# An attention and two-layer kernel: the low part of x for the first eight units formed by TensorE and ScalarE, its loads and first products in another order

## The chip, the cores and the metric

The kernel runs on one core of a Trainium2 chip (trn2). The metric is device time in microseconds (us) of one execution; lower is better. Engines are named as the profile names them: PE (TensorE matmul), PEld (its weight loads), DVE (VectorE), ACT (ScalarE), POOL (GpSimd), SP (SyncE, which here only issues DMAs).

## What is computed

The reference, cut to what matters: a gated linear attention over four batches, eight heads, 768 positions and a head size of 48; its 3072 rows of 384 go through two feed-forward layers of width 2048.

```
state = alpha[:, :, t, :, None] * state + einsum('bhd,bhe->bhde', k[:, :, t], v[:, :, t])
y[:, :, t] = einsum('bhd,bhde->bhe', q[:, :, t], state)
...
x = y.transpose(0, 2, 1, 3).reshape(3072, 384)
h = x @ w_in;  g = maximum(0.01 * h, h);  x = g @ w_out            # layer 1
h = x @ w_in;  g = where(h > 0, h, exp(minimum(h, 0)) - 1);  out = g @ w_out   # layer 2
```

## The kernel before, in words

**Units and blocks.** The attention is cut into 24 units of 128 positions, six per batch; four units make a block of 512 rows of `x`, so layer 1 works on six blocks. A product in this kernel takes its operands as a high part (fp32r) and a low part (what is left): `hp` is summed over `wh*xh`, `wl*xh` and `wh*xl`, nine matmuls of 512 columns, and `y` in the same way, nine matmuls from `gh` and `gl`.

**A unit** `u` is computed in four pieces (function `quarter(u, i)`):
- piece 0: PE `pu(u)` (L231); DVE `prep_k(u+1)`: scan `E` (L127), `pe`, reciprocal, product into `pack` (L132); DVE `T(u)` (L187).
- piece 1: DVE mask `A(u)` (L180, two); PE transposes `pk(u+1)` (L166), ACT copy `kn(u+1)` (L173); PE `po(u)` from `A` (L212) and from `T` (L218).
- piece 2: DVE scan `F(u+1)` (L139), `S(u)` (L248), product (L144); PE scores `sc(u+1)` (L158); ACT `xh(u)`, the high part of x out of the PSUM tile `po` (L237); the loads of `pack` and `vt` of unit `u+3`, issued on ACT's queue (L111, L116).
- piece 3: DVE `xl(u) = po - xh` (L240); after a block's last unit also `gather`, six DMAs on SP's queue (L262) that move rows of `x` into place, without which that block's `hp` cannot start.

`sc`, `pk`, `pu` and `po` share three PSUM buffers in turn (pool `ps_a`), so `pu(u+1)` takes the buffer of `po(u)` and waits for the last reader of `po(u)`.

**Weights of layer 1** arrive as 64-bit words and are converted, 16 slices `m`. `stage1(m)` asks for the words of one slice with five DMAs on SP's queue (786 KB in all) into one of four buffers. Conversion of a slice is `p` (ACT, L270 and L271), `a` (DVE L275, L276, L278, then ACT L279, the high part) and `b` (DVE L282, the low part; then `stage1(m+4)`).

**Order.** Up to the end of the sixteen steps below, every engine runs in the order in which the code is written. First come units 0 to 3 with the conversion of slices 0 to 2 among them, then the start of unit 4 with the first two `hp` of block 0. Then sixteen steps `s`: PE `y` of slice `s`, PE `hp` of slice `s+2`, ACT `t` (L303), conversion `a` of slice `s+3`, pieces of units 4 to 7, DVE `max` (L308), ACT `gh` (L312), conversion `b`, DVE `gl` (L318), conversion `p` of the next slice. Of the thirteen pieces left, one is placed in each of the steps 1 to 13. After step 15 the rest (blocks 1 to 5 of layer 1 with units 8 to 23, then layer 2) is ordered by the framework's scheduler.

Of the kernel before, what the change touches and what calls it, by code (L numbers as in the profile page):

```python
# [19 lines left out]
def attention_two_layers_kernel(  # L20
# [40 lines left out]

    ident = const.tile([128, 128], F32, name="ident")
    causal = const.tile([128, C], F32, name="causal")
    d0 = const.tile([PR, EXT], F32, name="d0")
    d1 = const.tile([PR, EXT], F32, name="d1")
    bias = const.tile([PR, 2], F32, name="bias")
# [16 lines left out]

    def constants():
        make_identity(nc, ident)
        nc.gpsimd.memset(causal, 1.0)
        nc.gpsimd.affine_select(
            out=causal, in_=causal, compare_op=ALU.is_ge, fill=0.0,
            base=0, pattern=[[1, C]], channel_multiplier=-1,
        )  # L90
        nc.vector.memset(d0, 0.0)
        nc.vector.memset(d0[:, 0:EXT:C + 1], 1.0)
        nc.vector.memset(d1, 0.0)
        nc.vector.memset(bias[:, 0:1], -1.0)
        nc.vector.memset(bias[:, 1:2], -ALPHA_SPAN)
        nc.vector.memset(far_sum[:, 1:2], 1.0)
# [141 lines left out]

    def attn_xl(u, xh, xl, off):
        nc.vector.tensor_sub(xl[0:PR, :, off:off + C], st[u]["po"], xh[0:PR, :, off:off + C].bitcast(F32))  # L240

    def attn_state(u):
        c = u % NC
# [57 lines left out]
    def ffn1_t(j, m):  # L301
        t = g_p.tile([128, xt[j][2]], F32, tag="t", name="t")
        nc.scalar.activation(t, steps[1, j, m], ACTF.Copy, scale=0.01)  # L303
        steps[1, j, m] = t, steps[1, j, m]

    def ffn1_max(j, m):
        t, hp = steps[1, j, m]
        nc.vector.tensor_max(t, t, hp)  # L308
# [140 lines left out]
    def next_load(u):  # L449
        if u < NU:  # L450
            load_unit(u, eng=nc.scalar)
            load_v(u, eng=nc.scalar)
        else:
            t = pack_p.tile([128, 2 * 768], I32, tag="pack", name="stg")
            slots2.extend([(t[:, 0:768], 99), (t[:, 768:1536], 99)])
            fill2()
# [3 lines left out]
    def stage1(m, eng=None):  # L460
        t = x2t[m % 4].rearrange("p c f -> p (c f)").bitcast(I32)
        w = w_words[0][m]
        n = 2 * DM
        for j in range(2):
            nc.sync.dma_start(t[64 * j:64 * j + D, 0:n], w[D * j:D * j + D, 0:n])
            nc.sync.dma_start(t[64 * j + D:64 * j + 64, 0:n], w[PD + 16 * j:PD + 16 * j + 16, 0:n])
        nc.sync.dma_start(t[:, n:], w[:, n:])
        staged[1, m] = t
# [184 lines left out]
    with ExitStack():  # L653
# [5 lines left out]
        load_v(1)  # L659
        stage1(0)  # L660
        load_v(2)
        for m in range(1, 4):
            stage1(m)
        order1 = [("both", m) for m in range(KF)]
        conv1 = Conversions(1, order1)
        conv2 = Conversions(2, order2)
# [4 lines left out]
        def quarter(u, i, chain=True):  # L671
            j = unit_block[u]
            xh, xl, _, t = xtile(j)
            off = (u - blocks[j][0]) * C
            if i == 0:
                attn_pu(u)
                prep_k(u + 1)
                attn_T(u)
            elif i == 1:
                attn_mask(u)  # L680
                if chain:
                    attn_pk(u + 1)
                    attn_kn(u + 1)
                attn_po(u)
            elif i == 2:
                prep_F(u + 1)
                attn_state(u)
                prep_q(u + 1)
                if chain:
                    attn_sc(u + 1)  # L690
                attn_xh(u, xh, off)
                next_load(u + 3)
            else:
                attn_xl(u, xh, xl, off)
                st.pop(u)
                if u == blocks[j][0] + blocks[j][1] - 1:
                    gather(t, blocks[j][1] * C)
# [5 lines left out]
        for u in range(UB):  # L703
            for i in range(3):
                quarter(u, i)
            if u > 1:
                conv1.a(u - 1)
            quarter(u, 3)
            if u > 1:
                conv1.b(u - 1)  # L710
            if u > 0:
                conv1.p(u)
# [2 lines left out]
        ffn1_h(0, 0)  # L715
        ffn1_t(0, 0)
        quarter(UB, 1)
        conv1.b(UB - 1)
        ffn1_max(0, 0)
        ffn1_gh(0, 0)  # L720
        quarter(UB, 2)
        ffn1_h(0, 1)
        ffn1_t(0, 1)
        ffn1_gl(0, 0)
        conv1.p(UB)
        ffn1_max(0, 1)
        ffn1_gh(0, 1)
        ffn1_gl(0, 1)
        in_order()

# [11 lines left out]
        for s, e in enumerate(seq):  # L742
# [3 lines left out]
            if s < KF:  # L746
                ffn1_y(j, m)
                pe_h(n)
                ffn1_t(n[1], n[2])
                conv1.a(s + 4)  # L750
                if s < KF - LA:
                    for p in quarters[13 * s // (KF - LA):13 * (s + 1) // (KF - LA)]:
                        quarter(*p, chain=p[0] + 1 < UB + blocks[1][1])
                ffn1_max(n[1], n[2])
                ffn1_gh(n[1], n[2])
                conv1.b(s + 4)
                ffn1_gl(n[1], n[2])
                conv1.p(s + 5)
                in_order()
                continue  # L760
# [127 lines left out]
```

## Time and profile before

| what | value |
|---|---|
| median of the runs shown | 975.14 us (974.55, 975.14, 976.91) |
| the profiled execution: time / span of its trace | 976.15 us / 974.4 us |
| PE busy | 922.9 us (95%) |
| DVE busy | 532.4 us (55%) |
| ACT busy | 445.9 us (46%) |
| DMA moved | 62.38 MB |

The span runs from the first to the last instruction; 1.75 us of the profiled execution's time lie outside it. The profiled execution is 1.0 us above the median of the three timed runs. Shares of the span are averages over stages; the stages are told apart below.

### The profile page before, as it was taken

The numbers are of one execution on the slowest core, as the hardware profiler recorded it, in microseconds if no ns is written. First come the engines' busy times: TensorE is split into PE (matmuls) and PEld (weight loads), VectorE is DVE, ScalarE is ACT, GpSimd is POOL, SyncE is SP. The second block draws the span as 40 slices with busy tenths as digits, with TensorE's granted clock in tenths as the row PEclk, the third lists the DMA queues.
The fourth block names the chain that finished last, engine by engine and source line by source line (L and its number), as shares of the span: only waits on it lengthen the run. The fifth ranks groups of instructions, "written<-read, shape, count | busy, mean of one in ns | idle before, by whom it ended". The sixth has DMA issues, their size and how long they took to land.

```text
span 974.4 us, 13128 instructions
## 1 busy us (share of the span) xinstructions
PE 922.9 (95%) x5234; PEld 779.2 (80%) x5234; DVE 532.4 (55%) x876; ACT 445.9 (46%) x783; POOL 1.1 (0%) x8
## 2 busy tenths in 40 slices
PE   5678889999999999999999999999999999999996
PEld 4555666888788788788888889999999999899995
DVE  6769894855746556545369993433433433433332
ACT  1235653322322222233367795474564654644442
POOL 0000000000000000000000000000000000000000
PEclk9688998999999999999999999999999999999998
DMA  9664523113111212211134430020110200100001
GB/s 247 161 160 135 165 74 89 42 41 90 49 41 42 57 41 83 57 41 49 33 114 133 127 90 18 1 81 1 47 34 1 71 10 1 62 1 0 33 1 37
DMA packets 25093, 62.38 MB, mean 64 GB/s; under 512 B 3936, under 2 KB 7008, under 8 KB 25024
## 3 DMA queue, kind: packets, MB, share of 16 engines
q1 hardware_dynamic: 19184, 40.54, 14.8%
q10 hardware_dynamic: 5840, 20.92, 7.7%
q8 instruction: 43, 0.70, 0.3%
q14 instruction: 26, 0.21, 0.1%
HBM read 54.37 MB, written 4.72 MB: 61 GB/s over the span
## 4 chain that ended last, share of the span: by engine, by line
PE 84%; DVE 6%; DMA 6%; issue 1%; SPq 1%; ACT 1%; DVEq 0%; ACTq 0%
PE hp L364 21%; PE y L335 18%; PE hp L297 18%; PE oa L395 10%; PE o L395 10%; DMA x2t<-in_w_dram 2%; PE sc L158 2%; PE po L212 2%; PE po L218 2%; DMA vt<-in_vals_dram 2%; DVE x2t L276 1%; DVE x2t L278 1%; DMA pack<-in_seqs_dram 1%; DMA x<-x 1%; DVE x2t L275 1%
## 5 line engine op out<-in xcount | busy, mean ns | idle before, releaser
L297 PE MATMUL hp<-x,w 128*128 128x512 f32 x864 | 219.6, 397 | 14.8 <-DMA x<-x 7.4
L364 PE MATMUL hp<-x,w 128*128 128x512 f32 x864 | 215.4, 393 | 0.0
L297 PEld LDWEIGHTS hp<-x,w 128*128 128x128 f32 x864 | 162.2, 190 | 54.3 <-DVE w L282 8.0
L364 PEld LDWEIGHTS hp<-x,w 128*128 128x128 f32 x864 | 160.7, 188 | 29.3
L335 PE MATMUL y<-gh,w 128*128 128x512 f32 x576 | 179.8, 400 | 0.0
L373 DVE SCALAR_TENSOR_TENSOR t<-t,hp 128x512 f32<-128x512 f32 x96 | 65.9, 686 | 148.1 <-ACT t L372 148.1
L335 PEld LDWEIGHTS y<-gh,w 128*128 128x128 f32 x576 | 106.9, 191 | 23.5 <-issue 1.1
L303 ACT ACTIVATE t<-hp 128x512 f32<-128x512 f32 x96 | 57.2, 596 | 125.8 <-PE hp L297 125.6
L312 ACT CAST gh<-t 128x512 fp32r<-128x512 f32 x96 | 59.6, 621 | 113.3 <-PE y L335 61.7
L335 PE MATMUL y<-gl,w 128*128 128x512 f32 x288 | 109.9, 395 | 0.0
L308 DVE TENSOR_TENSOR t<-t,hp 128x512 f32<-128x512 f32 x96 | 65.4, 681 | 78.6 <-ACT t L303 78.6
L81 DVE TENSOR_TENSOR gl<-t,gh 128x512 fp32r<-128x512 f32 x96 | 66.4, 692 | 70.6 <-ACT gh L78 68.9
L371 ACT ACTIVATE t<-hp 128x512 f32<-128x512 f32 x96 | 57.1, 595 | 104.7 <-PE hp L364 104.7
L395 PE MATMUL oa<-w,gh 128*128 128x384 f32 x384 | 96.7, 337 | 0.0
L395 PE MATMUL o<-w,gh 128*128 128x384 f32 x384 | 94.6, 336 | 0.0
L318 DVE TENSOR_TENSOR gl<-t,gh 128x512 fp32r<-128x512 f32 x96 | 66.1, 689 | 47.6 <-ACT gh L312 44.6
L78 ACT CAST gh<-t 128x512 fp32r<-128x512 f32 x96 | 59.5, 620 | 64.7 <-PE oa L395 34.8
L395 PEld LDWEIGHTS o<-w,gh 128*128 128x128 f32 x384 | 70.6, 188 | 5.4
L395 PEld LDWEIGHTS oa<-w,gh 128*128 128x128 f32 x384 | 70.2, 188 | 2.9
L335 PEld LDWEIGHTS y<-gl,w 128*128 128x128 f32 x288 | 54.5, 189 | 12.1
L395 PE MATMUL oa<-w,gl 128*128 128x384 f32 x192 | 63.0, 337 | 0.0
L372 ACT ACTIVATE t<-t 128x512 f32<-128x512 f32 x96 | 60.8, 633 | 2.3
(91 smaller groups left out, 833.0 us busy)
## 6 DMA issues: line engine op xcount, KB each, us to landing
pack<-in_seqs_dram ACTq DMA_DIRECT2D x21, 674.2 KB, 5.6
stg<-in_w_dram SPq DMA_DIRECT2D x28, 384.0 KB, 3.2
x2t<-in_w_dram SPq DMA_DIRECT2D x20, 384.0 KB, 3.8
vt<-in_vals_dram ACTq DMA_DIRECT2D x21, 288.0 KB, 5.6
span<-in_seqs_dram SPq DMA_DIRECT2D x24, 226.2 KB, 2.6
x2t<-in_w_dram SPq DMA_DIRECT2D x32, 144.0 KB, 2.8
out_dram<-osb SPq DMA_DIRECT2D x24, 192.0 KB, 2.1
x<-x SPq DMA_DIRECT2D x36, 64.0 KB, 4.4
```

The source lines that it names most:

```text
L78: nc.scalar.copy(dst, src)
L81: (lo_engine or nc.vector).tensor_sub(lo, src, dst.bitcast(F32))
L297: nc.tensor.matmul(hp, lhsT=a[:, kk, :], rhs=x[:, kk, :n], start=(i == 0), stop=(i == 3 * KD - 1))
L303: nc.scalar.activation(t, steps[1, j, m], ACTF.Copy, scale=0.01)
L308: nc.vector.tensor_max(t, t, hp)
L312: nc.scalar.copy(gh, steps[1, j, m][0])
L318: nc.vector.tensor_sub(gl, t, gh.bitcast(F32))
L335: nc.tensor.matmul(ytiles[j][c], lhsT=a[:, c * 128:(c + 1) * 128], rhs=x, start=(m == 0 and i == 0), stop=(m == KF - 1 and i == 2),)
L364: nc.tensor.matmul(hp, lhsT=a[:, kk, :], rhs=x[:, kk, :], start=(i == 0), stop=(i == 3 * KD - 1))
L372: nc.scalar.activation(t, t, ACTF.Exp, scale=-1.0)
L373: nc.vector.scalar_tensor_tensor(out=t, in0=t, scalar=-1.0, in1=hp, op0=ALU.add, op1=ALU.max)
L395: nc.tensor.matmul(otiles[j][i], lhsT=a[:, i * 128:(i + 1) * 128], rhs=x, start=(m == 0 and n == 0), stop=(m == KF - 1 and n == 2),)
```

## The change

Line numbers of the changed file are 2 to 10 higher than those of the kernel before (L237 becomes L239, L158 L160, L297 L306, L279 L288, L270 L279, L271 L280, L335 L344, L465 to L467 L474 to L476, L111 L113, L116 L118).

For units 0 to 7 the low part of `x` is no longer a subtraction on DVE. `attn_rest` lets PE add `minus * xh` to the tile `po` (one matmul, 112 by 112 by 512 columns, `minus` being the negative identity), so that `po` holds the rest, and ACT copies it into `xl`. The matmul stands in piece 2, behind `sc(u+1)`; the copy stands where DVE's subtraction stood, in piece 3. The loads of unit `u+3` move from ACT's queue to SP's. The words of slices 1 to 3 are no longer asked for at the start, but after piece 2 of the units 0 to 2. The second `hp` of block 0 comes before `b` of slice 2 and before piece 2 of unit 4. The thirteen pieces of units 4 to 7 stand in steps 0 to 12, one in each.

```
+    minus = const.tile([PR, PR], F32R, name="minus")
...
+        nc.scalar.activation(minus, ident[0:PR, 0:PR], ACTF.Copy, scale=-1.0)
...
+    def attn_rest(u, xh, off):
+        nc.tensor.matmul(st[u]["po"], lhsT=minus, rhs=xh[0:PR, :, off:off + C], start=False, stop=True,
+                         skip_group_check=True)
+
+    def attn_xl_act(u, xl, off):
+        nc.scalar.copy(xl[0:PR, :, off:off + C], st[u]["po"])
...
         stage1(0)
         load_v(2)
-        for m in range(1, 4):
-            stage1(m)
...
                 attn_xh(u, xh, off)
-                next_load(u + 3)
+                attn_rest(u, xh, off)
+                load_unit(u + 3)
+                load_v(u + 3)
             else:
-                attn_xl(u, xh, xl, off)
+                attn_xl_act(u, xl, off)
...
             for i in range(3):
                 quarter(u, i)
+            if u < 3:
+                stage1(u + 1)
...
         quarter(UB, 1)
+        ffn1_h(0, 1)
+        ffn1_t(0, 1)
         conv1.b(UB - 1)
+        quarter(UB, 2)
         ffn1_max(0, 0)
         ffn1_gh(0, 0)
-        quarter(UB, 2)
-        ffn1_h(0, 1)
-        ffn1_t(0, 1)
+        ffn1_max(0, 1)
+        ffn1_gh(0, 1)
         ffn1_gl(0, 0)
         conv1.p(UB)
-        ffn1_max(0, 1)
-        ffn1_gh(0, 1)
         ffn1_gl(0, 1)
...
-                if s < KF - LA:
-                    for p in quarters[13 * s // (KF - LA):13 * (s + 1) // (KF - LA)]:
-                        quarter(*p, chain=p[0] + 1 < UB + blocks[1][1])
+                for p in quarters[s:s + 1]:
+                    quarter(*p, chain=p[0] + 1 < UB + blocks[1][1])
```

On ACT, unit 2 in the first stretch: before, `xh(2)`, the two loads of unit 5, the high part of weight slice 0, then `p` of slice 1.

```order
L237 CAST x<-po 112x4x128
L111 DMA pack<-in_seqs_dram 112x1541
L116 DMA vt<-in_vals_dram 128x576
L279 CAST w_0_102<-x2t_138 128x768
L270 ACTIVATE x2t_139<-x2t_135 128x768
L271 ACTIVATE x2t_135<-x2t_135 128x768
```

The same place on ACT in the changed kernel.

```order
L239 CAST x<-po 112x4x128
L288 CAST w_0_103<-x2t_139 128x768
L249 CAST x<-po 112x4x128
L279 ACTIVATE x2t_140<-x2t_136 128x768
L280 ACTIVATE x2t_136<-x2t_136 128x768
```

The loads have left ACT, and the copy of the low part (L249) stands behind the high part of the weight slice (L288).

On PE, the step that holds piece 2 of unit 5: before, the last three matmuls of that step's `hp`, the eight score products of unit 6, then the next step's `y`.

```order
L297 MATMUL hp<-x,w_6_114 128x512 x3
L158 MATMUL sc_818<-pack 128x128
L158 MATMUL sc_819<-pack 128x128
L158 MATMUL sc_818<-pack 128x128
...
L158 MATMUL sc_819<-pack 128x128
L335 MATMUL y_599<-gh,w_5_112 128x512
L335 MATMUL y_599<-gh,w_5_113 128x512
```

The same place on PE in the changed kernel, which is one slice of the weights earlier.

```order
L306 MATMUL hp<-x,w_5_113 128x512 x3
L160 MATMUL sc_787<-pack 128x128
L160 MATMUL sc_788<-pack 128x128
L160 MATMUL sc_787<-pack 128x128
...
L160 MATMUL sc_788<-pack 128x128
L245 MATMUL po<-x,minus 112x512
L344 MATMUL y_606<-gh,w_4_111 128x512
```

The matmul with `minus`, which reads `xh`, now stands between the scores and the next `y`, and piece 2 of unit 5 stands with slice 5 instead of slice 6.

On SP's queue, behind the first load of `vt` for unit 2: before, the words of slices 1 and 2 follow.

```order
L467 DMA x2t_134<-in_w_dram 128x768
L116 DMA vt<-in_vals_dram 128x576
L465 DMA x2t_135<-in_w_dram 48x768
L466 DMA x2t_135<-in_w_dram 16x768
L465 DMA x2t_135<-in_w_dram 48x768
L466 DMA x2t_135<-in_w_dram 16x768
L467 DMA x2t_135<-in_w_dram 128x768
L465 DMA x2t_136<-in_w_dram 48x768
```

The same place on SP in the changed kernel.

```order
L476 DMA x2t_135<-in_w_dram 128x768
L118 DMA vt<-in_vals_dram 128x576
L113 DMA pack<-in_seqs_dram 112x1541
L118 DMA vt<-in_vals_dram 128x576
L474 DMA x2t_136<-in_w_dram 48x768
L475 DMA x2t_136<-in_w_dram 16x768
L474 DMA x2t_136<-in_w_dram 48x768
L475 DMA x2t_136<-in_w_dram 16x768
L476 DMA x2t_136<-in_w_dram 128x768
L113 DMA pack<-in_seqs_dram 112x1541
```

The loads of units 3 and 4 (L113, L118) now stand in SP's queue, each ahead of the next slice's words.

## Rows read from the trace of the kernel before

**Rows 1.** Windows: stretch, PE, PEld, DVE, ACT, POOL busy (instructions), clock, DMA share, GB/s

```profile
0.00:25.00 25.00, 12.90 (x122) 10.68 (x124) 16.74 (x32) 3.46 (x5) 1.14 (x8) 0.89 0.95 249
300.00:400.00 100.00, 100.00 (x640) 80.48 (x638) 56.21 (x92) 29.11 (x50) 0.00 (x0) 1.00 0.20 54
```

**Rows 2.** Timeline of DVE in the first stretch: start, duration, instruction, idle before

```profile
17.03 0.69 DVE L240 TENSOR_TENSOR x<-po,x 112x512 fp32r<-112x512 f32 x1 [2.48 <-ACT x L237]
...
30.08 1.23 DVE L127 TENSOR_TENSOR_SCAN E<-pack,d 112x517 f32<-112x517 f32 x1 [3.15 <-DMA pack<-in_seqs_dram]
...
32.49 1.28 DVE L180 TENSOR_TENSOR A<-sc,causal 128x512 f32<-128x512 f32 x2
...
40.17 1.23 DVE L127 TENSOR_TENSOR_SCAN E<-pack,d 112x517 f32<-112x517 f32 x1
...
48.40 0.68 DVE L240 TENSOR_TENSOR x<-po,x 112x512 fp32r<-112x512 f32 x1
```

**Rows 3.** Timeline of SP's queue: DMA issues

```profile
12.48 0.33 SPq L465 DMA_DIRECT2D x2t<-in_w_dram  x1
...
156.59 3.78 SPq L262 DMA_DIRECT2D x<-x  x6
```

**Rows 4.** Timeline of PE in the first stretch

```profile
17.78 0.67 PE L231 MATMUL pu<-vt,kn 128*64 128x48 f32 x16 [0.33 <-DVE x L240]
20.79 1.01 PE L166 MATMUL pk<-ident,pack 112*128 112x112 f32 x4 [2.34 <-DVE A L180]
...
25.50 2.08 PE L158 MATMUL sc<-pack 48*128 48x128 f32 x16
...
54.95 4.77 PE L297 MATMUL hp<-x,w 128*128 128x512 f32 x9 [5.15 <-DMA x<-x]
59.65 1.53 PE L212 MATMUL po<-A,vt 128*64 128x128 f32 x16
```

**Rows 5.** Windows of PE alone: stretch, PE busy, granted clock, DMA share, GB/s

```profile
18.00:21.00 3.00, 0.66 (x17) 0.77 1.02 256
...
70.00:74.00 4.00, 3.31 (x15) 1.00 0.09 23
...
90.00:93.00 3.00, 2.21 (x16) 0.50 0.45 137
```

**Rows 6.** Timeline of DVE in the sixteen steps

```profile
80.21 0.56 DVE L275 TENSOR_SCALAR x2t<-x2t 128x768 int32<-128x768 int32 x1
...
102.30 0.55 DVE L275 TENSOR_SCALAR x2t<-x2t 128x768 int32<-128x768 int32 x1
...
107.60 0.55 DVE L275 TENSOR_SCALAR x2t<-x2t 128x768 int32<-128x768 int32 x1
...
155.84 0.68 DVE L240 TENSOR_TENSOR x<-po,x 112x512 fp32r<-112x512 f32 x1
```

**Rows 7.** Timeline of ACT in the step with piece 2 of unit 5

```profile
99.33 0.60 ACT L303 ACTIVATE t<-hp 128x512 f32<-128x512 f32 x1 [5.23 <-PE hp L297]
...
99.83 0.82 ACT L279 CAST w<-x2t 128x768 fp32r<-128x768 f32 x1
100.55 0.59 ACT L237 CAST x<-po 112x512 fp32r<-112x512 f32 x1
```

**Rows 8.** Timeline of PE in the steps and at the start of block 1

```profile
97.09 2.20 PE L297 MATMUL hp<-x,w 128*128 128x512 f32 x9
99.22 1.16 PE L158 MATMUL sc<-pack 48*128 48x128 f32 x16
...
162.21 2.66 PE L297 MATMUL hp<-x,w 128*128 128x512 f32 x7 [0.76 <-DMA x<-x]
164.67 1.05 PE L335 MATMUL y<-gh,w 128*128 128x512 f32 x2
```

**Rows 9.** The page's costliest groups: count, busy us, mean ns, idle before

```profile
L312 ACT CAST gh<-t 128x512 fp32r<-128x512 f32 x96 | 59.6, 621 | 113.3 <-PE y L335 61.7
...
L318 DVE TENSOR_TENSOR gl<-t,gh 128x512 fp32r<-128x512 f32 x96 | 66.1, 689 | 47.6 <-ACT gh L312 44.6
```

## The prediction

> **What bounds the kernel now.** I read the windows first. From about 165 us to the last matmul PE is busy without a gap (100.00 of 100 us in the window shown), while in the first 25 us it is busy for 12.90 [rows 1]; nobody waits inside the later stretch for anything that the change touches. So PE's remaining work is a fixed block, and the change is worth what it moves the start of that block. The block starts with the `y` of the last slice of block 0 at 164.67, right after the `hp` of block 1 that waited for `gather` [rows 8]. The question is when that `y` starts afterwards.
>
> Then the timelines of DVE and PE up to 165 us. The reader should see three stretches: units 0 to 3 (to about 50 us), the start of block 0 (`hp` from 54.95 [rows 4]), and the sixteen steps, where the conversions and unit pieces on DVE set the pace and the step with piece 2 waits for PE. They end with DVE's L240 of unit 7 at 155.84, then `gather` at 156.59 [rows 3, 6].
>
> **Units 0 to 3: about 8 us earlier.** Today DVE stands still twice: 2.48 us for ACT's `xh(0)` before L240, and 3.15 us for the `pack` of unit 3 before the scan at 30.08 [rows 2]. Both go. L240 leaves DVE, so the scan for unit 2 can follow the product before it, at 14.55 (17.03 less the wait) instead of behind L240 at 17.6. The `pack` of unit 3 takes the place in SP's queue at which slice 1 is asked for now, 12.48 [rows 3]. At the 249 GB/s of the first 25 us [rows 1] the 4.4 MB asked for up to and with it (four packs of 690 KB, three `vt` of 295 KB and one slice, by the sizes of the tiles) need 17.8 us, so it lands near 19, before it is wanted.
>
> New in this stretch: `pu(1)` takes the buffer of `po(0)`, so it waits for `xh`, the new matmul and ACT's copy, instead of `xh` and L240. One matmul of 512 columns costs 0.25 us (a ninth of the 2.20 of nine [rows 8]), a copy of this shape 0.59 [rows 7]; behind the scores `sc(1)` that puts `pu(1)` near 18.4 instead of 17.78 [rows 4]. `A(1)` runs at about 17.5 to 18.8, `F(2)`, `S(1)` and the product to 20.8, then the scan for unit 3 at 20.8, 9.3 us ahead of its 30.08. `A(2)` waits for the scores `sc(2)`, and here the price hangs on TensorE's clock. It was granted 0.77 in 18 to 21 us and one half after that, when PE had stood idle for 2.34 us before 20.79 [rows 4, 5]; the scores then took 2.08 instead of 1.16 [rows 4, 8]. With the change PE stands idle for 0.7 us only before `pu(1)`. In 70 to 74 us, where PE was idle for 0.69, the clock stayed full [rows 5]. If it stays full here, `pk`, `po` and the scores of unit 2 end near 23, and `A(2)` starts at 23.3 instead of 32.49: 9.2 earlier. If it falls as before, they end near 25.5 (7.0 earlier), and L279 behind `xh(2)` costs some 0.5 more: 6.5. What follows up to the scan at 40.17 [rows 2] is DVE's own work, the same as now: between L278 and L282 DVE waits for L279 in any case, and L240 lay in that gap, so its 0.69 us is not saved there. I take 8.0, nearer to the full clock.
>
> Sums of this kind need the loads to keep up. Seven packs and `vt`s and five slices, 10.8 MB, must be through before the first `gather`, 43 us at 249 GB/s. It starts near 42. That is close, and goes into the range; the words for each slice arrive several us before their `p`.
>
> **End of unit 3: 0.85 us back.** `xl(3)`, which `gather` waits for, was DVE's L240 at 48.40, ending 49.08 [rows 2], beside L279. Now ACT does L279 first and the copy after it: 0.82 + 0.59 after L278 instead of 0.69, with the hand-overs some 0.85 later.
>
> **Start of block 0 to the first step with piece 0 of unit 5: 6.3 us earlier.** Now from 54.95 to 80.21 [rows 4, 6], 25.3 us, because a step with piece 3 of unit 4 lies between. Afterwards, chained: `hp` 4.8 [rows 4], `po(4)` 2.5 (1.53 [rows 4] and its second part), the second `hp` 2.3, `t` 0.6, `xh(4)` 0.6 [rows 7], `gh` 0.6, `gl` 0.7 [rows 9], seven matmuls of `y` 1.6, `hp` of slice 2 2.2 [rows 8], `t` 0.6, then L279, the copy, `gh` and `gl` 2.5: 19.0. DVE's `F`, `S` and product of unit 5 now run while PE is at the `hp`s, so `max` finds them done.
>
> **The steps: 7.05 us back.** From L275 at 80.21 to `gather` at 156.59 [rows 3, 6] lie 76.4 us, with three units' pieces 0, 1, 2 and two pieces 3 that carry a conversion (102.30 to 107.60 is one, 5.30 us [rows 6]); the third, in step 13, has none and takes 0.75 to `gather`. Afterwards the same units lie in steps 1 to 12. Pieces 0 and 1 have the same DVE work. In piece 2 the new matmul waits for `xh`, which on ACT stands behind `t` and L279: `hp` ends at 99.29, `xh` at 101.14 [rows 7, 8]. The scores end at 100.3; the new matmul then ends near 101.4, so `y` of the next step starts 1.1 us later than now. In the next step `y` and `hp` (2.2 each) and `t` end at 106.4 rather than 105.3, and DVE, through with `a` at about 104.9 (the step's 5.30 less L240, `max`, L282 and `gl`, 0.6 to 0.9 each), waits 1.5 us for it. L279, the copy and `gh` then follow one another on ACT, `gl` after them: that step lasts 6.55 instead of 5.30. So 1.25 more for each of units 5 and 6. The third piece 3 now shares step 12 with a conversion: `hp` behind the late matmul, `t`, L279 and the copy put `gather` 5.3 us after the step's start instead of 0.75, 4.55 more. Sum 2.5 + 4.55 = 7.05.
>
> **`gather` and block 1.** `gather` needs 5.6 us from its first issue to the last `hp` part that waited for it (156.59 to 162.21 [rows 3, 8]). By then PE has the two steps behind it done 1.2 us earlier, so `gather` still ends last and the block starts with the same distance: 0.
>
> Edits with no term: building `minus` lies 9 us before its use; the eight new matmuls are priced where they stand; loads off ACT's queue free nothing that ACT waits for in these rows, since its compute goes on beside them. What queues behind SP's waits for a buffer (`pack` of `u+3` waits for PE's `po(u)`) is the next slice's words, needed three steps later.
>
> **Sum.** 8.0 - 0.85 + 6.3 - 7.05 = 6.4 us. The profiled execution (976.15, of which the span is 974.4) would become 969.75; it stood 1.0 above the median, so the median 975.14 becomes 968.7. With the clock's two ends the gain is 4.9 to 7.6.
>
> A rule bears on the loads. The rows show one queue (SP's, between 12 and 22 us) filling the DMA engines: their share is 1.02 in 18 to 21 us at 256 GB/s [rows 5]. The Trainium skill ("DMA: Bandwidth & Descriptors", section "Issuing engines are not separate DMA queues") says that DMAs from several engines end up on the same 16 DMA engines and that issuing from more than one only saves issue time. By that, moving loads to SP's queue costs no bandwidth, and the trace agrees. The same page (section "Queues, rings and completion order") says that each DMA engine alternates between queue rows but takes one row's descriptors in order. By that `gather` would no longer share with a load ahead of it but stand behind it; no run here shows it yet, and it is the second rival below.
>
> **Rivals.**
> - *PE's clock falls in the steps (slower).* The new wait of about 0.9 us in each piece 2 comes one step after piece 1, where PE already waits, and where the clock has been seen at one half (90 to 93 us [rows 5]). Nine matmuls took 4.77 at one half [rows 4] and 2.20 at full clock [rows 8], so a following `y` and `hp` at one half cost up to 5.1 more; at 3.9, since part of it would recover, for each of three units it is 11.7, which gives 968.7 + 11.7 = 980.4. It decides from 2.1 us per unit on. Against it: the clock recovered by itself after such a fall, and 0.69 us of idle left it full. Chance 0.08.
> - *`gather` and words stand behind the loads (no change).* With the loads of units 6 and 10 ahead in the same queue, 985 KB or 3.9 us at 249 GB/s each, the first `gather` could end up to 3.9 later; the load is asked for about 2.5 us ahead of it, so 1.5 is likely left, but a stretch of DMAs behind time adds to it. Gain 6.4 - 3.9 = 2.5: 972.6. For the second `gather` the load is some 8 us ahead and gone. Against it: `gather` takes 3.8 us to issue [rows 3], which covers most of such a wait. Chance 0.14.
> - *The clock stays full and PE is quick from the start (a little faster than forecast).* 967.5 to 966: as above with 9.2, and a shorter low clock after the last `gather`. Chance 0.2, inside the range.
> - *Forecast*, 966.5 to 971: chance 0.58.
>
> **How the numbers follow.** The likeliest is 968.7. Upwards the range takes in the `gather` rival at 972.6; downwards the full clock and one us for the slow matmuls after the second `gather` (1.05 for two at 164.67 [rows 8]): 965.5. Outside stay the clock rival and half of what lies beyond either end, under 0.2. About 0.3%, 2.9 us, is what a measurement of this kernel can tell from no change: faster than 972.2 takes forecast and full clock, 0.78; within 0.3% most of the `gather` rival, 0.14; slower the clock rival, 0.08.
>
> **What would show it.** Right: the scan of unit 3 near 21 with no wait for `pack`; no DVE wait for `xh`; the first `hp` between 47 and 51; the new matmul in each piece 2 waiting about 0.9 us for ACT; `max` in the step after it waiting for `t`; the second `gather` near 150; PE without gaps from about 158. Wrong: the scan of unit 3 waiting for a load; `hp` of block 0 starting after 52; the clock at one half in the steps with piece 3; conversions waiting for words.

## The result, and the profile after

The changed kernel takes 965.59 us (median of 4 runs, 964.51 to 966.01) beside 974.86 for the kernel before (974.55 to 976.91): a ratio of 0.9899, 95% interval 0.9882 to 0.9916, so about 9.3 us faster. The prediction of 968.7 had the sign, but the time lies just below its low end (965.5, where the ratio puts the kernel at 965.3 of the 975.14 shown).

The head of the page of the changed kernel; compare the table of the kernel before: PE's busy time is nearly the same, on a span 10.4 us shorter.

```profile
span 964.0 us, 13162 instructions
PE 921.6 (96%) x5242; PEld 777.9 (81%) x5242; DVE 528.2 (55%) x868; ACT 449.3 (47%) x792; POOL 1.1 (0%) x8
```

DVE's timeline of the changed kernel, units 0 to 3 (against [rows 2]), and one step with piece 3:

```profile
18.86 1.29 DVE L182 TENSOR_TENSOR A<-sc,causal 128x512 f32<-128x512 f32 x2 [1.46 <-PE sc L160]
...
22.05 1.23 DVE L129 TENSOR_TENSOR_SCAN E<-pack,d 112x517 f32<-112x517 f32 x1
...
25.19 1.29 DVE L182 TENSOR_TENSOR A<-sc,causal 128x512 f32<-128x512 f32 x2 [0.65 <-PE sc L160]
...
32.87 1.23 DVE L129 TENSOR_TENSOR_SCAN E<-pack,d 112x517 f32<-112x517 f32 x1
...
66.37 0.56 DVE L284 TENSOR_SCALAR x2t<-x2t 128x768 int32<-128x768 int32 x1
...
92.39 0.69 DVE L317 TENSOR_TENSOR t<-t,hp 128x512 f32<-128x512 f32 x1 [1.43 <-ACT t L312]
...
142.86 0.56 DVE L284 TENSOR_SCALAR x2t<-x2t 128x768 int32<-128x768 int32 x1
```

The scan of unit 3 (22.05) no longer waits for its `pack`, the one of unit 4 starts at 32.87 instead of 40.17, and the masks wait for the scores by 1.46 and 0.65 us only. The line at 92.39 is the predicted wait for `t`.

SP's queue of the changed kernel (against [rows 3]): the `pack` of unit 3, then the two `gather`s.

```profile
12.63 0.33 SPq L113 DMA_DIRECT2D pack<-in_seqs_dram  x1
...
42.55 3.94 SPq L271 DMA_DIRECT2D x<-x  x6
...
149.80 3.80 SPq L271 DMA_DIRECT2D x<-x  x6
```

PE's timeline of the changed kernel (against [rows 4, 8]): the scores `sc(1)`, the first `hp`, the new matmul (L245) of units 5 and 7, and the work around the second `gather`.

```profile
16.75 2.08 PE L160 MATMUL sc<-pack 48*128 48x128 f32 x16
...
47.72 4.56 PE L306 MATMUL hp<-x,w 128*128 128x512 f32 x9 [4.47 <-DMA x<-x]
...
87.13 0.49 PE L245 MATMUL po<-x,minus 112*112 112x512 f32 x1 [0.80 <-ACT x L239]
...
141.75 0.67 PE L245 MATMUL po<-x,minus 112*112 112x512 f32 x1 [1.89 <-ACT x L239]
142.22 1.05 PE L344 MATMUL y<-gh,w 128*128 128x512 f32 x2
...
155.43 1.83 PE L306 MATMUL hp<-x,w 128*128 128x512 f32 x7 [0.78 <-DMA x<-x]
157.09 0.62 PE L344 MATMUL y<-gh,w 128*128 128x512 f32 x2
...
159.13 2.20 PE L306 MATMUL hp<-x,w 128*128 128x512 f32 x9
```

Here the reader sees what was not foreseen. The last `hp` parts of the second `gather` end their wait 5.63 us after its first issue (155.43 less 149.80), as before (5.62 [rows 3, 8]). But the seven matmuls behind the wait take 1.83 instead of 2.66, and the two of the first `y` 0.62 instead of 1.05. PE's clock says why; first PE's windows of the changed kernel (PE busy, granted clock, DMA share, GB/s), then the stretch of the kernel before that answers to the third, and last PE's timeline of the kernel before around its second `gather`, the rows beside those of [rows 8].

```profile
18.00:21.00 3.00, 2.92 (x27) 1.00 1.04 248
...
143.00:147.00 4.00, 4.00 (x14) 0.71 0.00 0
159.00:162.00 3.00, 3.00 (x20) 1.00 0.00 0
```

```profile
162.00:165.00 3.00, 2.79 (x8) 0.66 0.66 241
```

```profile
159.68 0.47 PE L297 MATMUL hp<-x,w 128*128 128x512 f32 x1 [0.68 <-DMA x<-x]
...
160.99 0.47 PE L297 MATMUL hp<-x,w 128*128 128x512 f32 x1 [0.84 <-DMA x<-x]
...
167.55 0.63 PE L297 MATMUL hp<-x,w 128*128 128x512 f32 x2
```

Before, PE stood idle for 0.68, 0.84 and 0.76 us around two single matmuls while `gather` landed, and the granted clock of the next 3 us was 0.66: part of them at the lower of its two levels (1.2 of 2.4 GHz). Now PE is still at its steps when `gather` lands, and waits once.

The window of 18 to 21 us cannot be read in the same way. Its clock is given as 1.00, but `sc(1)`, which ends in it, took 2.08 us, as the scores at 25.50 did in the kernel before [rows 4] while the clock was given as 0.50; at full clock they take 1.16 [rows 8]. So by the durations PE still ran at the lower level here.

By the prediction's marks, start times before less after, from the two profiled executions (a second trace of the changed kernel, `changed_again` below, has other shares):

| stretch | predicted | measured |
|---|---|---|
| up to the scan of unit 4 (40.17, 32.87) | +8.0 | +7.30 |
| from there to the first `gather` (49.11, 42.55) | -0.85 | -0.74 |
| `gather` to the first `hp` (54.95, 47.72) | 0 | +0.67 |
| to the step with piece 0 of unit 5 (80.21, 66.37) | +6.3 | +6.61 |
| to the second `gather` (156.59, 149.80) | -7.05 | -7.05 |
| to the `hp` behind the next `y` (167.55, 159.13) | 0 | +1.63 |
| sum | 6.4 | 8.42 |

From that `hp` on PE's work is the same within 0.2 us up to its last matmul (965.14 before, 956.56 after). Another 1.8 of the spans' 10.4 lie in the tail behind it, from the start of PE's last row to the end of the span: 9.26 us before, 7.44 after. PE's last row, and how long SP's queue then stood still (us in total, times, longest), before and after:

```profile
965.14 0.69 PE L395 MATMUL oa<-w,gl 128*128 128x384 f32 x3
SPq L802 <- SPq L802: 4.5, 2, 2.7
```

```profile
956.56 0.69 PE L404 MATMUL oa<-w,gl 128*128 128x384 f32 x3
SPq L812 <- SPq L812: 2.6, 1, 2.6
```

At its very end SP stands still once less, 2.6 us in all instead of 4.5. This is no accident of two executions: the tail is 9.2 to 9.7 us in all five traces of kernels that load units 3 to 10 on ACT's queue, and 7.4 to 7.9 in all nine that load them on SP's. So it goes with the loads edit; why it does is open.

### The profile page after: what moved, and what is told of

The parts are those of the page before. It is cut to its first block, busy times and chain, and to the rows that moved or that the text cites. A ratio compares the mean times of both kernels' runs of the same rounds, so it can differ in the third digit from the quotient of the medians.

```text
span 964.0 us, 13162 instructions
## 1 busy us (share of the span) xinstructions
PE 921.6 (96%) x5242; PEld 777.9 (81%) x5242; DVE 528.2 (55%) x868; ACT 449.3 (47%) x792; POOL 1.1 (0%) x8
## 4 chain that ended last, share of the span: by engine, by line
PE 91%; DVE 4%; DMA 2%; ACT 1%; issue 1%; SPq 0%; DVEq 0%
PE hp L373 21%; PE y L344 20%; PE hp L306 20%; PE oa L404 10%; PE o L404 10%; PE po L214 3%; PE sc L160 3%; PE po L220 2%; DMA x2t<-in_w_dram 1%; PE pk L168 1%; PE pu L233 1%; DVE x2t L287 1%; DMA x<-x 1%; DVE E L129 0%; ACT t L312 0%
## 5 line engine op out<-in xcount | busy, mean ns | idle before, releaser
L306 PE MATMUL hp<-x,w 128*128 128x512 f32 x864 | 218.7, 396 | 11.5 <-DVE w L291 5.8
L306 PEld LDWEIGHTS hp<-x,w 128*128 128x128 f32 x864 | 162.8, 190 | 49.1 <-DVE w L291 7.1
L344 PE MATMUL y<-gh,w 128*128 128x512 f32 x576 | 179.0, 398 | 0.0
L344 PEld LDWEIGHTS y<-gh,w 128*128 128x128 f32 x576 | 106.3, 189 | 23.1 <-issue 1.1
L344 PE MATMUL y<-gl,w 128*128 128x512 f32 x288 | 109.8, 394 | 0.0
L344 PEld LDWEIGHTS y<-gl,w 128*128 128x128 f32 x288 | 54.4, 189 | 12.3 <-DVE gl L327 0.4
```

The costliest lines, as they stand in the source:

```text
L306: nc.tensor.matmul(hp, lhsT=a[:, kk, :], rhs=x[:, kk, :n], start=(i == 0), stop=(i == 3 * KD - 1))
L344: nc.tensor.matmul(ytiles[j][c], lhsT=a[:, c * 128:(c + 1) * 128], rhs=x, start=(m == 0 and i == 0), stop=(m == KF - 1 and i == 2),)
```

## Experiments

The before-kernel that ran beside them had medians of 975.46 (the first four), 976.3 (the next four) and 976.88 (the last four).

**pieces_only: the kernel before with one piece a step.**

```
-                if s < KF - LA:
-                    for p in quarters[13 * s // (KF - LA):13 * (s + 1) // (KF - LA)]:
+                for p in quarters[s:s + 1]:
```

> The kernel before with one part of the change alone: the thirteen pieces stand in steps 0 to 12. My account by stages: nothing moves before 70 us; the scan for unit 6 comes about 4.7 us earlier (step 1 has no L240 any more and one step less lies ahead of piece 0 of unit 5); the last piece 3 then shares step 12 with a conversion, so its gather comes about 3.2 us after that step's start instead of 0.75. Net the second gather is some 2 us earlier, and 2 to 3.5 us faster in all, the more the less the clock falls at the wait for gather (about 972). Rival, that the place of the pieces is what the change lives on: 6 us or more faster. Rival, that 13 conversions on DVE set the end anyway: within 1 us of before.

970.88 us, ratio 0.9956 (0.9939 to 0.9972): 4.3 us faster, more than expected. In the trace the step with piece 0 of unit 5 starts 20.1 us after the first `hp` instead of 25.26 [rows 4, 6], the second `gather` 79.11 after that step instead of 76.38, and no `hp` waits for it: the next `hp` starts 9.38 us after its issue, not 10.96. The excess of about 1.6 is that last term, and it belongs to this edit.

**loads_only: the kernel before with the loads on SP's queue and the words asked for in turn.**

```
+                load_unit(u + 3)
+                load_v(u + 3)
-                next_load(u + 3)
...
+            if u < 3:
+                stage1(u + 1)
-        for m in range(1, 4):
-            stage1(m)
```

> The kernel before with the loads alone changed: pack and vt of unit u+3 on SP's queue, the words of slices 1 to 3 asked for one slice a unit. My account by stages: the pack of unit 3 lands before 20 us, so the 3.15 us of DVE's wait before the scan of unit 3 goes, but DVE still waits for xh(0) and xh(1) before L240; everything after is 3 us earlier and otherwise the same: about 3 us faster (972). Rival, that the loads are the whole of the first stretch's gain: 7 us faster. Rival, that gather stands behind the loads in SP's queue: the first gather takes longer than its 5.8 us, and the gain is under 1 us.

969.98, ratio 0.9945 (0.9928 to 0.9963): 5.4 us faster. The scan of unit 4 starts 3.07 us earlier, as expected, and the rest is later: the step with piece 2 of unit 5 lasts 7.49 instead of 9.08. This time the first `hp` came 7.60 us after `gather`'s first issue (before: 5.84), with a `pack` asked for 1.46 us ahead of it in the same queue. The three waits at the second `gather` stay (0.69, 0.85, 0.77), and so do 10.69 us from it to the next `hp`. The tail is 7.94 us instead of 9.26: that is 1.3 of the 5.4, and my account had no term for it.

**low_part_only: the kernel before with the low part on PE and ACT.**

```
+                attn_rest(u, xh, off)
...
-                attn_xl(u, xh, xl, off)
+                attn_xl_act(u, xl, off)
```

> The kernel before with the low part alone changed: matmul with minus and ACT's copy in place of DVE's subtraction, loads on ACT's queue and pieces where they were. My account by stages: the scan of unit 3 still waits for its pack, which lands at 30 us, so nothing is gained there; xl(3) ends 0.85 later; each step with a piece 3 takes 1.25 longer behind the late matmul, and the last gather comes 2 to 4 us later. So 4 to 7 us slower (979 to 982). Rival, that taking 0.69 us a unit off DVE is the source of the gain: 3 us or more faster.

983.58, ratio 1.0083 (1.0061 to 1.0106): 8.1 us slower. DVE's timeline of this run in units 2 and 3:

```profile
14.92 1.23 DVE L129 TENSOR_TENSOR_SCAN E<-pack,d 112x517 f32<-112x517 f32 x1
...
29.19 1.24 DVE L129 TENSOR_TENSOR_SCAN E<-pack,d 112x517 f32<-112x517 f32 x1 [7.04 <-DMA pack<-in_seqs_dram]
...
39.98 1.23 DVE L129 TENSOR_TENSOR_SCAN E<-pack,d 112x517 f32<-112x517 f32 x1
```

The scan of unit 2 starts early, and the wait for `pack` swallows all of it. The steps pay the price all the same: 83.31 us from the step with piece 0 of unit 5 to the second `gather`, where they were 76.38. That alone is 6.9 us, the top of the 4 to 7 expected; the 8.1 of the time lie above it.

**low_part_back: the changed kernel with DVE's subtraction back.**

```
-                attn_rest(u, xh, off)
...
-                attn_xl_act(u, xl, off)
+                attn_xl(u, xh, xl, off)
```

> The changed kernel with the low part alone put back: DVE's subtraction, no matmul with minus, no copy on ACT (the loads, the first products and the pieces as changed). My account by stages: DVE waits for xh(0) and xh(1) again, so the scan of unit 4 comes some 4 to 5 us later than with the change; xl(3) 0.85 sooner; the two steps with piece 3 take 5.3 instead of 6.5, and the last gather comes 2 us sooner after its step's start. Net within 1.5 us of the changed kernel (964 to 967). Rival, that the low part on PE and ACT carries the gain: 4 us or more slower than the changed kernel (970 or more).

965.82, ratio 0.9898 (0.9877 to 0.9918): as the changed kernel. The scan of unit 4 starts at 36.87, 4.0 later than in it, and the same stretch of steps takes 80.33 instead of 83.43 (5.7 later and 80.33 for 81.11 against the second trace, `changed_again`). So by the times the low part's new place pays for itself within the change; a gain or loss of a microsecond or two would not be seen.

**first_products_back: the changed kernel with the old start of block 0.**

```
-        ffn1_h(0, 1)
-        ffn1_t(0, 1)
         conv1.b(UB - 1)
-        quarter(UB, 2)
         ffn1_max(0, 0)
         ffn1_gh(0, 0)
-        ffn1_max(0, 1)
-        ffn1_gh(0, 1)
+        quarter(UB, 2)
+        ffn1_h(0, 1)
+        ffn1_t(0, 1)
         ffn1_gl(0, 0)
```

> The changed kernel with the start of block 0 alone put back: max and gh of the first hp ahead of piece 2 of unit 4, the second hp behind it. My account by stages: units 0 to 3 as in the changed kernel; from the first hp to the step with piece 0 of unit 5 it takes about 20.5 instead of 18.65 us, since DVE waits again for t ahead of F, S and the product of unit 5; the rest the same. About 2 us slower than the changed kernel (967 to 968). Rival, that ACT and PE bound this stretch in either order: the same as the changed kernel within 0.5 us.

967.94, ratio 0.9916 (0.9885 to 0.9947). The step with piece 0 of unit 5 starts 19.96 us after the first `hp` instead of 18.65, so 1.3 of the 2 us expected are seen there (2.2 against the 17.74 of `changed_again`); the times alone can't be told from those of the changed kernel.

**filled_wait: the kernel before with 12 matmuls of 512 columns, whose result nobody uses, on PE where it waits for the second `gather`.**

```
                 ffn1_y(j, m)
+                if m == 14:
+                    fill = ps_a.tile([128, 512], F32, tag="at", name="fill")
+                    for i in range(12):
+                        nc.tensor.matmul(fill, lhsT=win[0][0][:, 0, :], rhs=xt[0][0][:, 0, :], start=True, stop=True)
                 pe_h(n)
```

> The kernel before with 12 matmuls of 512 columns added on PE between the y of slice 14 and the first hp of block 1, where PE waits 2.3 us in three parts for gather; their result is used by nothing. If the clock that falls there is what makes the seven matmuls and the y behind gather slow (2.46 and 2.88 us instead of 1.66 and 2.04 in the changed kernel), the clock stays full through 168 us in the trace, these take 1.6 and 2.1, and PE's gapless stretch starts about 1.6 us earlier behind gather than in the kernel before. If the clock is not the cause, the stretch starts at the same distance behind gather, or up to 0.5 later if the added matmuls outlast the wait. The time itself would move by 1.6 at most, near what can be told apart.

PE's timeline of this run behind its second `gather`, which was issued at 156.12:

```profile
158.36 2.88 PE L751 MATMUL fill<-x,w 128*128 128x512 f32 x12
161.08 2.52 PE L297 MATMUL hp<-x,w 128*128 128x512 f32 x9
163.44 0.62 PE L335 MATMUL y<-gh,w 128*128 128x512 f32 x2
...
165.49 2.20 PE L297 MATMUL hp<-x,w 128*128 128x512 f32 x9
```

```profile
162.00:165.00 3.00, 3.00 (x14) 1.00 0.54 213
```

With nothing changed but that PE is kept busy, the clock stays full and the next `hp` starts 9.37 us after `gather`'s issue, 1.59 less than before and within 0.04 of the changed kernel's 9.33. The time itself, 974.77 with a ratio of 0.9992 (0.9973 to 1.0012), can't be told from that of the kernel before, nor from one 1.6 us less; the term is shown by the trace, not by the time.

**xh_ahead: the changed kernel with `xh` of units 5 to 7 asked of ACT ahead of that step's `t` and L288.**

```
                 pe_h(n)
+                for u, i in quarters[s:s + 1]:
+                    if i == 2:
+                        attn_xh(u, xtile(1)[0], (u - blocks[1][0]) * C)
                 ffn1_t(n[1], n[2])
```

> The changed kernel with xh of units 5 to 7 asked of ACT ahead of that step's t instead of behind t and the high part of the weights, so that the matmul with minus finds it done. My account by stages: the waits of PE before that matmul (0.80 and 1.89 us for units 5 and 7) go; the step with piece 3 of unit 5 lasts some 0.8 less, unit 6 is as before (there the scores wait for DVE), and after unit 7 the y that ran at half clock runs at full clock, which with the wait is 3.2 us. About 3 to 4 us faster than the changed kernel (962). Rival, that DVE's own work sets these steps and PE's wait is slack: within 1 us of the changed kernel. Rival, that gather or PE behind it takes the gain back: within 1 us, with the gather earlier.

961.86, ratio 0.9856 (0.9823 to 0.989). PE's timeline of this run, piece 2 of unit 7:

```profile
134.75 2.20 PE L306 MATMUL hp<-x,w 128*128 128x512 f32 x9
136.79 0.40 PE L245 MATMUL po<-x,minus 112*112 112x512 f32 x1
137.02 0.63 PE L344 MATMUL y<-gh,w 128*128 128x512 f32 x2
```

The new matmul follows `hp` directly, where it waited for 1.89 us above. The steps with piece 3 last 6.08 and 5.76 us (6.49 and 6.85 in the changed kernel), and the second `gather` comes 4.10 after the start of its step instead of 6.94.

**xl_in_piece_2: xh_ahead, with the copy of the low part in piece 2 and `gather` a step earlier.**

```
+                if early:
+                    attn_xl_act(u, xl, off)
+                    if u == blocks[1][0] + blocks[1][1] - 1:
+                        gather(t, blocks[1][1] * C)
```

> As the run with xh ahead, and for units 5 to 7 ACT copies the low part in piece 2, behind the matmul, so that the steps of piece 3 hold a conversion alone and the second gather is asked for one step earlier. My account by stages: steps of piece 3 at 4.7 to 5 us (DVE's conversion, max and gl) instead of 6.5 to 6.9; the first hp of block 1 no longer waits for gather (0.78 now). About 2 to 3 us faster than with xh ahead alone (959 to 960), 5.5 to 6.5 faster than the changed kernel. Rival, that the steps are bound by PE from here on: as with xh ahead alone.

961.39, ratio 0.9844 (0.981 to 0.9877); it can't be told from xh_ahead. The steps with piece 3 last 5.19, as without the copy, and no `hp` waits for the second `gather` any more; the next limit is the steps' own work.

**words_in_turn and loads_on_sp: meant as the two halves of loads_only.** The first keeps the loads on ACT's queue, the second keeps all words at the start.

> The kernel before with one half of the loads edit: the words of slices 1 to 3 are asked for in turn, the loads of units stay with ACT's queue. Theory (the gain of the loads edit comes from the order of the requests: pack of unit 3 is no longer asked for behind 15 requests for words): that pack is asked for near 17 us instead of 21.88, the scan for unit 3 starts near 26.8 without a wait for it, the scan for unit 4 near 37, the first gather is 5 to 6 us from the hp that waits for it, and the kernel is about 3 us faster than before. Rival (the queue matters, since ACT's compute stands behind its own requests): pack of unit 3 still arrives near 30 and the time stays.

> The kernel before with the other half of the loads edit: the loads of units are asked for by SP, the words of slices 1 to 3 still all at the start. Theory (order of the requests): pack of unit 3 stands behind the 15 requests for words in SP's own queue, is asked for near 22 us, the scan for unit 3 waits for it until about 30, and the time is that of before within 1.5 us. Rival (the queue matters): the scan for unit 3 starts near 27 and the kernel is 3 us faster.

words_in_turn: 976.79, ratio 0.9994 (0.998 to 1.0008). loads_on_sp: 973.09, ratio 0.9976 (0.9958 to 0.9994).

words_in_turn does not do what it was meant to. With the loads on ACT's queue nothing stands between the words in SP's, so SP asks for the words of slices 1 to 3 in one row, as before. The first and the last of these requests in words_in_turn:

```profile
10.92 0.33 SPq L465 DMA_DIRECT2D x2t<-in_w_dram  x1
...
19.27 0.42 SPq L467 DMA_DIRECT2D x2t<-in_w_dram  x1
```

In the kernel before, the first stands at 12.48 [rows 3]; the last of them, and behind it ACT's request for the `pack` of unit 3:

```profile
21.56 0.42 SPq L467 DMA_DIRECT2D x2t<-in_w_dram  x1
```

```profile
21.88 0.32 ACTq L111 DMA_DIRECT2D pack<-in_seqs_dram  x1
```

SP's requests are the same and in the same order in both traces. So this run is the kernel before once more, its time says so, and it tests neither theory. ACT in words_in_turn:

```profile
16.40 0.58 ACT L237 CAST x<-po 112x512 fp32r<-112x512 f32 x1 [1.32 <-PE po L212]
19.82 0.32 ACTq L111 DMA_DIRECT2D pack<-in_seqs_dram  x1
...
21.87 0.53 ACT L173 COPY kn<-pk 128x448 f32<-128x448 f32 x1 [4.89 <-DMA x2t<-in_w_dram]
```

The `pack` of unit 3 is asked for at 19.82, right behind the last request for words (19.27), though `xh(0)` ends at 16.98. In all five traces with the loads on ACT's queue it goes off 0.3 to 0.6 us after that last request starts. What holds it until then is open. The copy `kn` does not show it: it reads `pk`, which PE ends at 21.78, and it comes after 4.88 us of idling in loads_on_sp too, where ACT has no loads. DVE in loads_on_sp:

```profile
28.98 1.24 DVE L127 TENSOR_TENSOR_SCAN E<-pack,d 112x517 f32<-112x517 f32 x1 [2.73 <-DMA pack<-in_seqs_dram]
```

There the `pack` stands behind the words in SP's own queue (asked for at 20.60), and the wait stays, as the order of the requests would have it. Of the 2.3 us by which this kernel is faster, 1.5 lie in the tail (7.74 us for 9.26). Of the traces with DVE's subtraction, loads_only and low_part_back have the `pack` ahead of the words (asked for at 12.02 and 11.79), and only in these two the scan of unit 3 does not wait. So the order fits all of them, but no run changed the order alone.

The traced execution of words_in_turn took 971.15, the fastest of its twelve, with the scan of unit 3 at 27.46 instead of 30.08. Since it is the kernel before, its twelve times (971.15 to 977.63) show how far that kernel moves by itself.

**changed_again and xh_ahead_again: the changed kernel and xh_ahead once more, side by side.**

> The changed kernel once more, beside the one with xh asked for ahead: 965.6 within 1 us; second gather to the next hp near 9.3 us, with at most one part of hp waiting for gather.

> The changed kernel with xh of units 5 to 7 asked of ACT ahead of that step's t, once more: 3 to 4 us below the changed kernel on the same chip if the wait of the new matmul for xh is what it takes away; rival (spread of the first stretch): no difference between the two.

964.61, ratio 0.9884 (0.9859 to 0.9909), and 961.76, ratio 0.9853 (0.9827 to 0.9878): 2.9 us apart, as the first time within 1 us, with intervals that overlap. Asking for `xh` earlier most likely makes the kernel faster still; xh_ahead and xl_in_piece_2 are clearly faster than the kernel before. PE in changed_again, piece 2 of unit 7, the wait for the second `gather` (issued at 146.53) and the `hp` behind it:

```profile
140.07 0.48 PE L245 MATMUL po<-x,minus 112*112 112x512 f32 x1 [1.89 <-ACT x L239]
140.39 0.64 PE L344 MATMUL y<-gh,w 128*128 128x512 f32 x2
...
152.15 1.85 PE L306 MATMUL hp<-x,w 128*128 128x512 f32 x7 [0.77 <-DMA x<-x]
...
155.88 2.20 PE L306 MATMUL hp<-x,w 128*128 128x512 f32 x9
```

Again 9.35 us from `gather` to that `hp`. The other terms moved. In the first stretch of changed_again, PE and DVE:

```profile
16.38 1.49 PE L160 MATMUL sc<-pack 48*128 48x128 f32 x16
```

```profile
17.90 1.29 DVE L182 TENSOR_TENSOR A<-sc,causal 128x512 f32<-128x512 f32 x2 [0.87 <-PE sc L160]
...
21.09 1.23 DVE L129 TENSOR_TENSOR_SCAN E<-pack,d 112x517 f32<-112x517 f32 x1
...
31.18 1.23 DVE L129 TENSOR_TENSOR_SCAN E<-pack,d 112x517 f32<-112x517 f32 x1
```

By the marks of the table this trace gives, against the same trace of the kernel before, +8.99, -0.74, -0.98, +7.52, -4.73 and +1.61, in sum 11.67 where the first gave 8.42. Only the second and the last term are the same in both.

The traced execution of xh_ahead_again took 966.39, with 966.45 the longest of its six: in it the scan of unit 3 waits 1.57 us for its `pack`, and in xl_in_piece_2 1.75.

Over all traces, the stretch from the second `gather` to that `hp` sorts by one edit:

| kernels | second `gather` to that `hp`, us |
|---|---|
| one piece a step: the changed kernel (twice), pieces_only, low_part_back, first_products_back, xh_ahead (twice) | 9.32 to 9.38 |
| old places of the pieces: before, loads_only, words_in_turn, loads_on_sp, low_part_only | 10.69 to 11.33 |
| old places, PE kept busy: filled_wait | 9.37 |

xl_in_piece_2 is left out, since its `gather` comes a step earlier. In pieces_only and low_part_back no `hp` waits for `gather` either, so their 9.38 and 9.36 are PE's own work.

## Why the prediction was right in its sign and too small

**Half right: what bounds the kernel.** From the `hp` behind the second `gather` to PE's last matmul lie 797.6 us before and 797.4 after: PE's remaining work is a fixed block, as said. That "the change is worth what it moves the start of that block" does not follow and was wrong: the tail behind the last matmul became 1.8 us shorter, and it had no term. It goes with the queue of the loads in all fourteen traces.

**Right in mechanism, the size a matter of the execution: units 0 to 3.** Both waits went, the scan of unit 3 came at 22.05 (forecast 20.8), and 7.30 of the 8.0 came. The price hung on TensorE's clock, as said, but earlier than I looked: the first mask waited 1.46 us because `sc(1)` ran at the lower level (2.08 us). In changed_again it took 1.49, and 8.99 came. Over the six traces whose code is that of the changed kernel up to the scan of unit 4, this scan starts at 30.90 to 33.41, the two latest where the scan of unit 3 waits for its `pack` after all; over the four with the code of the kernel before, at 37.51 to 40.17, and the trace shown has the 40.17. So any pair of traces gives 4.1 to 9.3, and that 7.30 is near 8.0 is in part luck. low_part_only shows that the gain needs the loads edit (a 7.04 us wait for `pack` took its place).

**Right: the start of block 0 and the steps.** +6.61 for 6.3 (+7.52 in the second trace). The -7.05 of the steps came exactly, but as a sum of misses that cancel: the steps with piece 3 took 6.49 and 6.85 (forecast 6.55), `gather` came 6.94 after the start of its step (forecast 5.3), and against that the step with piece 2 of unit 6 took 6.69 where it had taken 8.16. In changed_again the same stretch took 81.11 (-4.73) and that last part 5.35. So this term moves by some 2 us from execution to execution, and the exact hit is luck.

**Wrong: "so `gather` still ends last and the block starts with the same distance: 0".** The first half held (5.63 for 5.62 us up to the last part that waited). The distance did not: PE has not done "the two steps behind it" when `gather` is issued, it is still in them, so two of its three waits fall away and the clock no longer falls; that is 1.63 us (1.61 in changed_again), and filled_wait gives the same 1.59 without touching `gather`. I had the slow matmuls in view only as one us for the low end of the range. That low end was also added up wrongly: 968.7 less 1.2 for the full clock and 1.0 for these matmuls is 966.5, not 965.5.

**The sum.** The forecast was 6.4. The distance (1.6) and the tail (1.8), two terms put at nothing, came in both traces of the changed kernel, and together they are 3.4 us, about what the forecast fell short by (968.7 for 965.59). In the two traces compared, the first `gather` was also 0.67 shorter, and the other terms came out 0.3 lower than forecast together. The 0.67 varies by itself (3.8 to 7.6 us over all traces from issue to the first `hp`; 5.17 and 6.82 in the two of the changed kernel, 5.84 before) and cannot be credited to the change. The interval of the timed gain is 8.2 to 11.5 us.

**The rivals.** The fall of the clock in the steps came once in the first trace (0.71 in 143 to 147 us behind the 1.89 us wait) and cost 1.6, the difference of 6.94 and 5.35; far from the 11.7. That `gather` stands behind the loads fits loads_only (7.60), but not the first trace of the changed kernel (5.17, with its last load asked for 2.3 us ahead). The Trainium skill ("DMA: Bandwidth & Descriptors", section "Queues, rings and completion order") says that each DMA engine takes the descriptors of one ring in order; these two values neither refute it nor show that it costs this kernel anything, since kernels with all loads on ACT lie between them (5.84 in the kernel before, 6.43 in words_in_turn). Over all traces with the loads on SP's queue, the first `gather` takes 6.2 to 7.6 us where the last load is asked for 1.3 to 1.5 us ahead of it (three traces), 5.2 to 6.8 at 2.2 to 2.4 (three) and 3.8 to 6.1 at 3.3 (three): the nearer load goes with the longer `gather`, within a spread as wide.

**Which edit is worth what.** Alone on the kernel before: one piece a step 4.3 us (interval 2.7 to 6.0), the loads 5.4 (3.6 to 7.0), the low part -8.1 (-6.0 to -10.3). Taken back from the whole, the low part is worth nothing that can be told, and the order of the first products 1.3 to 2.2 by the traces. The edits don't add up: the new place of the low part gains in units 0 to 3 only if the loads keep up, and costs in the steps in any case.

## What to carry to other kernels

A wait that stays as long as it was can still become cheaper: look at what PE does in it, since here the matmuls behind it were priced by the clock that the wait left. Look behind the last matmul too, even if nothing there is edited. Before an experiment is read, see in its trace that the edit moved what it was meant to move: words_in_turn moved nothing. And take each term of a sum from more than one trace of each kernel. When a step is moved from one engine to another, ask at once whether its input is made early enough in the new engine's order; here the new matmul waited for an `xh` that ACT made behind two other things, and asking for it first is most likely worth some 3 us more. Price edits together where one takes away the wait that would swallow the other's gain.

## What the runs showed of the hardware that was not expected

- Idle time in short pieces lowers the clock too: 0.68, 0.84 and 0.76 us with a single matmul between them were followed by a granted clock of 0.66 over 3 us. The Trainium skill ("TensorE: Matmul & The Clock Gate", section "HAM oscillation — how this bites in real kernels") describes matmul groups that start cold behind each wait for a DMA, at the cost of the slow matmuls that follow; the trace agrees, with shorter waits than the page's, and filled_wait, which fills the wait, shows what it costs here (1.59 us).
- The same wait need not lower it: behind 1.89 us of idling for `xh` the two matmuls of `y` took 1.05 us in three traces (the first of the changed kernel, low_part_only, first_products_back) and 0.64 in the fourth (changed_again), at the same place of the program.
- The arrival of a load decides several us of a run's time: with the loads of the kernel before, the `pack` of unit 3 let its scan start between 27.4 and 30.1 us, and in the six traces with the changed first stretch between 20.8 and 23.3.
- ACT's request for the `pack` of unit 3 went off only when a row of requests on SP's queue was through: at 21.88 behind 21.56, at 19.82 behind 19.27, and so in all five traces with these loads on ACT's queue. Nothing in the `pack` itself asks for that: SP asks for the same one at 12.63 in the changed kernel.
- The end of the program, behind the last matmul, took 9.2 to 9.7 us or 7.4 to 7.9, and the fourteen traces sort by the queue on which the loads of units 3 to 10 were asked for, more than 800 us earlier.
